# The first token group of a fused attention and MoE kernel: two products in plain float32 on whole weights, the fp32r halves of the weights made later, and conversion and loads spread anew

## Chip, cores and metric

One core of a Trainium2 chip runs the whole program. The metric is the device time of one execution in microseconds (us). The kernel before has a median of 759.26 us over three runs (758.15 to 760.97).

## What is computed

Three layers in a row, for 2 x 768 tokens of 8 heads of 64, that is 1536 tokens of width 512:

```python
scores = scale * np.matmul(q, k.transpose(0, 1, 3, 2))          # causal window of 128, and 4 sinks
a = np.exp(scores - max); a = a / (a.sum() + 1e-9); x = a @ v    # attention

r = np.maximum(x @ w_in, 0.0)                                    # dense layer, 512 -> 2048 -> 512
x = (r * r) @ w_out

logits = x @ w_gate + np.log1p(np.exp(x @ w_noise)) * noise      # top 2 of 8 experts
out[mask] += weight * (np.maximum(x[mask] @ w1[e], 0.0) @ w2[e]) # 512 -> 1024 -> 512
```

`w_in` and `w_out` come as float64. The kernel has to make float32 of them on the chip, out of the integer words.

## The kernel before

The 1536 tokens are six groups of 256. `fast1` does attention and the dense layer, the class `Experts` the rest. Inside both the order of the instructions on each engine is the order of the code (`manual_schedule`): every engine takes its own instructions one after the other and waits at each for what it needs.

**The prologue** goes over the heads a = 0 to 10 (group 0 has heads 0 to 7, group 1 starts with 8). For each head `scores` (L237, plain float32, two matmuls) is followed by `soft`: the VectorE (DVE) adds the mask and takes the minimum (L255), the ScalarE (ACT) takes exp with its sum (L258). `norm_a` adds 1e-9 (L262) and takes the reciprocal (L264), `norm` multiplies (L276 on DVE, L274 on ACT; strings such as "da" say which engine takes which of the two tiles). `trans` turns the tile on the TensorE (PE), `trans_b` copies it out on ACT, `pv` multiplies with v (L313) for two heads at a time, and ACT copies the result to `xraw` (L315). In the text "the soft row" of a head or step is its first L255 row on DVE, which comes as soon as its scores are there and DVE is free. `keep_warm` puts some matmuls without a use between (L653).

**Steps n = 0 to 47** then interleave attention of head a = n + 11 with the dense layer: step n belongs to group g = n // 8 and weight part u = n % 8. In a step PE does in this order: `scores(a)`, `pv(n + 8)` if n is even, the first product `mm1(n + 1)` (L383), the transposes `trans(n + 10)`, the second product `mm2(n)` (L416). Where u = 7, `mm2(n)` comes ahead of the scores, since the next group's input has to be split first (`split_x`, L366 on ACT and L367 on DVE). `act` (ACT) takes relu and square of the first product's result, `act_b` (L403, L404) the rest of the square that the fp32r tile has lost.

**fp32r in three passes.** A product of two float32 tiles is made of three fp32r matmuls: high x high, high x rest, rest x high (`PASS`). So each weight lies in SBUF as a high half and a rest, in one tile `w` [128, 2, 1024] of a ring of 16: eight parts u of `win` and of `wout`. The ring's tiles are used again for the experts' weights from step 40 on. `prep` splits q and k in the same way from head 18 on (`qs`, `kk`; casts on ACT at L214 and L215, subtractions on DVE at L216 and L217); the 18 heads before take plain float32.

**Conversion.** `cv_load` loads half a weight part as integer words (`st`, 512 KB, three buffers, queue of SP). Three DVE instructions make float32 of it: "1" (L171), "2" (L174), "3" (L177). "H" then makes the two halves: the high one on ACT (L148), the rest on GpSimd (POOL, L149). The tables `C0` (prologue) and `C1` (steps 0 to 7) say where in a head or step each of these letters stands. Of the 32 half parts 11 and two thirds are converted in the prologue. In steps 0 to 5 POOL also makes the rest of the square.

From step 8 on, `range_load` reads the float64 weights once more in 32 pieces, one per step, into two buffers `rw`, and `range_check` takes a minimum of each. The experts' raw weights use the same two buffers later.

Of the kernel before, what the change touches and what calls it, by code (L numbers as in the profile page):

```python
# [26 lines left out]
C = 448  # L27
# [7 lines left out]
def build(tc, io):  # L35
# [3 lines left out]
    with root:  # L39
# [3 lines left out]
        ring = rst.enter_context(tc.tile_pool(name="ring", bufs=16))  # L43
        rgt = ExitStack()
        xg = dram.tile([XROWS, TR], F32, name="xg")
# [50 lines left out]
def fast1(tc, io, env):  # L96
    nc = tc.nc
    PE, ACT, DVE, POOL, SP = nc.tensor, nc.scalar, nc.vector, nc.gpsimd, nc.sync
    wk, ps, ring, consts = env["wk"], env["ps"], env["ring"], env["consts"]
# [52 lines left out]
    nxt, whole, split = {"1": 0, "2": 0, "3": 0}, [], set()  # L152

    def convert(todo):

        for c in todo:
            if c == "H":
                while whole:
                    cv_b(whole.pop(0))
                continue  # L160
# [6 lines left out]
            if c == "1":  # L167
                if hf == 0:
                    W[name, u] = ring.tile([128, 2, 1024], F32R, name="w")
                t = CV[i] = cvp.tile([128, 512], I32, name="cv", bufs=4)  # L170
# [4 lines left out]
            else:  # L175
                t = CV[i]
                DVE.scalar_tensor_tensor(t, wd[:, :, 0], 29, t, op0=OP.logical_shift_right, op1=OP.bitwise_or)  # L177
                CV[i] = t.bitcast(F32)
                del ST[i]
                whole.append(i)  # L180
# [120 lines left out]
    def pv(a):  # L301
# [3 lines left out]
        if h == 0:  # L305
# [68 lines left out]
    def mm1(n):  # L374
        g, u = divmod(n, 8)
        assert ("win", u, 1) in split
        x, w = XT[g], W["win", u]
        hp = ps.tile([128, 2, 256], F32, name="h")
        for f in range(2):
            i = 0  # L380
            for c in range(4):
                for a, b in PASS:
                    PE.matmul(hp[:, f], w[:, a, c * 256 + f * 128:c * 256 + f * 128 + 128], x[:, b, c],  # L383
# [4 lines left out]
    def act(n, first=False):  # L388
        hp = HP.pop(n)
        r = wk.tile([128, 512], F32, name="r", bufs=1)  # L390
        gt = wk.tile([128, 2, 512], F32R, name="gt", bufs=2)
# [6 lines left out]
        GT[n] = gt, r, first  # L398

    def act_b(n):  # L400
        gt, r, first = GT[n]
        if not first:
            DVE.tensor_tensor(r, r, r, op=OP.mult)  # L403
        (POOL if first else DVE).tensor_tensor(gt[:, 1], r, gt[:, 0].bitcast(F32), op=OP.subtract)  # L404
        GT[n] = gt

    def mm2(n):
# [3 lines left out]
        assert ("wout", u, 1) in split  # L411
        gt, w = GT.pop(n), W["wout", u]
        for f in range(2):
            for t in range(2):
                for i, (a, b) in enumerate(PASS):
                    PE.matmul(ACC[g][t], gt[:, a, f * 256 + t * 128:f * 256 + t * 128 + 128],  # L416
                              w[:, b, f * 512:f * 512 + 512],
# [172 lines left out]
    def a_mm1(u, half):  # L590
# [5 lines left out]
        for c in range(4):  # L596
            for a, b in PASS:
                PE.matmul(hp[:, f], w[:, a, c * 256 + f * 128:c * 256 + f * 128 + 128], x[:, b, c],
# [10 lines left out]
    def a_mm2(u):  # L609
# [3 lines left out]
        for f in range(2):  # L613
            for t in range(2):
                for i, (a, b) in enumerate(PASS):
                    PE.matmul(A["acc"][t], hh[:, a, f * 256 + t * 128:f * 256 + t * 128 + 128],
                              w[:, b, f * 512:f * 512 + 512],
# [16 lines left out]
    C0 = (("1", "", "2", ""),) + (("H31", "", "2", ""),) * 9 + (("H31", "", "2", "H132"),)  # L634
    H0, H1, H2 = "da", "ad", "dd"
    STEP = "3", "1", "2H", "132132"
    C1 = (STEP,) * 3 + (STEP[:3] + ("132132132",),) + (STEP,) * 2 + (("3", "1", "2H", "3H"),) * 2
    smv = {}
    HALF, V1 = 8, (2, 3, 4)
    W0, W1 = 8, (3,) * 6 + (2,) * 5  # L640

    with tc.manual_schedule():
# [15 lines left out]
        cv_load()  # L658
        cv_load()
        scores(0, True)  # L660
        make_masks()
        for a in range(A0):
# [8 lines left out]
            if a == 0:  # L671
                load_v(0)
                cv_load()
# [6 lines left out]
            if a == 8:  # L680
                split_x(0)
            if a + 1 < A0:
                trans(a)
            convert(C0[a][3])
            if a == 9:
                mm1(0)
            if a == 10:
                act(0, True)
# [12 lines left out]
        for n in range(48):  # L701
# [7 lines left out]
            if n == 8:  # L709
# [7 lines left out]
                ex.range_load(1)  # L717
            if g >= 1 and u == 0:
                rows(p)
            if first:  # L720
                convert("H")
# [593 lines left out]
```

## Time and profile before

The profiled execution took 761.03 us; its span, which the trace covers, is 759.2 us.

| stretch, us from the span's start | what | PE busy | DVE busy | POOL busy |
|---|---|---|---|---|
| 0 to 49.29 | prologue | 38.74 | 38.68 | 17.24 |
| 49.29 to 125.05 | steps 0 to 6, and the second product of 7 | 64.81 | 74.57 | 52.35 |
| 125.05 to 169.46 | step 7 to the first product in step 13 | 44.07 | 30.57 | 4.54 |
| 169.46 to 189.12 | to the first product in step 15 | 19.66 | 15.13 | 4.25 |
| 189.12 to 759.2 | groups 2 to 5, experts | 556.16 | 312.81 | 96.88 |

A stretch in which one engine is busy for nearly its whole length is set by that engine, as long as no other one makes it wait. Busy time is not work alone: an instruction that is held up while it runs counts as busy.

### The profile page before, as it was taken

The numbers are of one execution on the slowest core, as the hardware profiler recorded it, in microseconds if no ns is written. First come the engines' busy times: TensorE is split into PE (matmuls) and PEld (weight loads), VectorE is DVE, ScalarE is ACT, GpSimd is POOL, SyncE is SP. The second block draws the span as 40 slices with busy tenths as digits, with TensorE's granted clock in tenths as the row PEclk, the third lists the DMA queues.
The fourth block names the chain that finished last, engine by engine and source line by source line (L and its number), as shares of the span: only waits on it lengthen the run. The fifth ranks groups of instructions, "written<-read, shape, count | busy, mean of one in ns | idle before, by whom it ended". The sixth has DMA issues, their size and how long they took to land.

```text
span 759.2 us, 12296 instructions
## 1 busy us (share of the span) xinstructions
PE 723.4 (95%) x4448; PEld 638.9 (84%) x4448; DVE 471.8 (62%) x1156; ACT 352.6 (46%) x741; POOL 175.3 (23%) x313
## 2 busy tenths in 40 slices
PE   7878879999999999999999999999999999999995
PEld 3467657988888888888898878899999999999994
DVE  6899998677768768766464445544554445455511
ACT  3675556564565555555254415333344433334410
POOL 1377563112002102301202022201112030303032
PEclk6799999999999999999999999999999999999998
DMA  8765576855756422622325027635556464646233
GB/s 230 222 207 179 191 250 221 280 198 175 246 169 227 167 101 96 215 94 84 114 84 170 1 91 240 210 111 156 141 160 156 148 169 134 172 137 165 74 43 46
DMA packets 37734, 119.05 MB, mean 157 GB/s; under 512 B 5038, under 2 KB 5166, under 8 KB 37408
## 3 DMA queue, kind: packets, MB, share of 16 engines
q1 hardware_dynamic: 31584, 104.37, 41.9%
q0 software_dynamic: 5792, 13.28, 8.5%
q8 instruction: 37, 0.61, 0.3%
q10 hardware_dynamic: 288, 0.52, 0.2%
q14 instruction: 33, 0.27, 0.1%
HBM read 104.88 MB, written 24.91 MB: 171 GB/s over the span
## 4 chain that ended last, share of the span: by engine, by line
PE 75%; DVE 12%; DMA 5%; issue 3%; ACT 2%; POOL 1%; SPq 0%; DVEq 0%; POOLq 0%; ACTq 0%
PE h L1001 18%; PE h L383 12%; PE acc L416 12%; PE acc L1027 7%; PE s L1027 7%; DVE cv L177 3%; PE o L313 2%; PE acc L1024 2%; PE s L241 2%; PE s L1024 1%; DVE cv L174 1%; DVE cv L171 1%; DMA xg<-xr,sx 1%; DVE pr L255 1%; DMA qk<-in_qk 1%
## 5 line engine op out<-in xcount | busy, mean ns | idle before, releaser
L416 PE MATMUL acc<-w,gt 128*128 128x512 f32 x576 | 149.5, 408 | 12.1 <-POOL gt L404 8.6
L383 PE MATMUL h<-xt,w 128*128 128x256 f32 x1152 | 148.9, 285 | 1.8 <-POOL w L149 1.5
L383 PEld LDWEIGHTS h<-xt,w 128*128 128x128 f32 x1152 | 140.5, 188 | 6.6 <-issue 3.2
L416 PEld LDWEIGHTS acc<-w,gt 128*128 128x128 f32 x576 | 106.5, 192 | 38.2 <-POOL gt L404 10.7
L1001 PE MATMUL h<-xt,w 128*128 128x448 f32 (+6 forms) x672 | 134.4, 349 | 0.0
L1001 PEld LDWEIGHTS h<-xt,w 128*128 128x128 f32 x672 | 123.3, 188 | 3.0
L906 DVE TENSOR_TENSOR w<-rw,w 128x1024 fp32r<-128x1024 f32 x64 | 78.4, 1225 | 37.7 <-ACT w L905 37.6
L1008 DVE SCALAR_TENSOR_TENSOR hh<-h,hh 128x256 fp32r<-128x256 f32 (+7 forms) x60 | 33.9, 565 | 108.1 <-ACT hh L1007 106.7
L1007 ACT ACTIVATE hh<-h 128x256 fp32r<-128x256 f32 (+7 forms) x60 | 29.8, 496 | 148.4 <-PE h L1001 148.4
L258 ACT ACTIVATE pr<-pr,mxall 128x264 f32<-128x264 f32 (+1 forms) x96 | 46.8, 489 | 74.5 <-DVE mxall L255 69.3
L975 POOL DMA_INDIRECT out<-x2t,mi x15 | 22.7, 1515 | 235.3 <-DVE x2t L1052 235.3
L1027 PE MATMUL acc<-hh,w 128*128 128x448 f32 (+5 forms) x288 | 72.7, 360 | 0.0
L905 ACT CAST w<-rw 128x1024 fp32r<-128x1024 f32 x64 | 67.1, 1049 | 10.1 <-DMA rw<-in_w 10.1
L1027 PE MATMUL s<-hh,w 128*128 128x448 f32 (+5 forms) x288 | 69.8, 350 | 0.0
L392 ACT ACTIVATE r<-h 128x512 f32<-128x512 f32 x48 | 28.6, 595 | 62.2 <-PE h L383 59.0
L149 POOL TENSOR_TENSOR w<-cv,w 128x512 fp32r<-128x512 f32 x32 | 45.8, 1432 | 47.5 <-ACT w L148 46.5
L1027 PEld LDWEIGHTS s<-hh,w 128*128 128x128 f32 x288 | 53.4, 188 | 1.2
L282 POOL COPY psk<-pr 128x8 f32<-128x8 f32 x64 | 23.8, 375 | 127.7 <-DVE pr L276 123.0
L1027 PEld LDWEIGHTS acc<-hh,w 128*128 128x128 f32 x288 | 51.1, 188 | 1.1
L255 DVE CUSTOM_DVE_ANT_0 pr<-s,masks 128x264 f32<-128x264 f32 (+1 forms) x96 | 35.4, 403 | 23.1 <-PE s L241 19.1
L403 DVE TENSOR_TENSOR r<-r 128x512 f32<-128x512 f32 x41 | 28.3, 690 | 28.7 <-ACT gt L397 28.7
L547 POOL DMA_INDIRECT xg<-xr,sx x24 | 26.1, 1086 | 43.0 <-DVE r L403 18.4
(238 smaller groups left out, 1084.0 us busy)
## 6 DMA issues: line engine op xcount, KB each, us to landing
rw<-in_w SPq DMA_DIRECT2D x64, 512.0 KB, 3.4
qk<-in_qk SPq DMA_DIRECT2D x40, 328.0 KB, 4.8
st<-in_win SPq DMA_DIRECT2D x16, 512.0 KB, 3.9
st<-in_wout SPq DMA_DIRECT2D x16, 512.0 KB, 4.5
rw<-in_win SPq DMA_DIRECT2D x16, 512.0 KB, 4.4
rw<-in_wout SPq DMA_DIRECT2D x16, 512.0 KB, 4.0
xg<-in_xg SPq DMA_DIRECT2D x8, 924.0 KB, 6.0
xr<-xg SPq DMA_DIRECT2D x24, 231.0 KB, 4.6
```

Source lines behind the costliest of these rows:

```text
L149: POOL.tensor_tensor(w[:, 1, sl], tf, w[:, 0, sl].bitcast(F32), op=OP.subtract)
L255: DVE.tensor_tensor_reduce(pt, SB[a][t][:, lo:hi], masks[:, t if gl == 0 else 2 + t, lo:hi], scale=-0.0625 if a in PLAIN and a >= HALF els ...
L258: ACT.activation(pt, pt, AF.Exp, bias=mx, scale=-1.0, accum_out=sm[:, t:t + 1])
L383: PE.matmul(hp[:, f], w[:, a, c * 256 + f * 128:c * 256 + f * 128 + 128], x[:, b, c], start=i == 0, stop=i == 11)
L392: ACT.activation(r, hp.rearrange("p a b -> p (a b)"), AF.Relu)
L416: PE.matmul(ACC[g][t], gt[:, a, f * 256 + t * 128:f * 256 + t * 128 + 128], w[:, b, f * 512:f * 512 + 512], start=u == 0 and f == 0 and i ...
L905: nc.scalar.copy(w[:, 0], t)
L906: nc.vector.tensor_tensor(w[:, 1], t, w[:, 0].bitcast(F32), op=OP.subtract)
L1001: PE.matmul(hp[:, :ncol], w[:, a, o:o + 128], XT[k][:, b, c, :ncol], start=i == 0, stop=i == 11)
L1007: ACT.activation(hh[:, 0, :ncol], hp[:, :ncol], AF.Relu)
L1008: DVE.scalar_tensor_tensor(hh[:, 1, :ncol], hp[:, :ncol], 0.0, hh[:, 0, :ncol].bitcast(F32), op0=OP.max, op1=OP.subtract)
L1027: PE.matmul(acc[:, :n], w[:, a, o + j * 128:o + j * 128 + 128], hh[:, b, :n], **st)
```

## The change

- In group 0 (steps 0 to 7) `mm1` and `mm2` take plain float32 operands: the whole weights `RAW`, the attention output `xraw[0]` and a float32 `gt`. The compiler makes two PE instructions of each such matmul. `split_x(0)`, the rest of the square and its third ACT instruction are gone in this group. `xraw[0]` lies in the buffer of `xt`.
- The ring's tiles are two, `w` (high) and `wl` (rest) of [128, 1024], 16 each. The converted weights lie in `wl` tiles (the last of them in a new buffer `spare`). `half_1` makes the high half on ACT at the end of steps 0 to 7, one instruction for a whole part, two a step. `half_2` makes the rest on DVE at the end of steps 6 to 13, two a step. POOL makes no halves any more.
- Conversion: two of the three DVE letters per head in the prologue (three in heads 9 and 10), twelve per step in steps 0 to 5, none later. `st` has four buffers, and four pieces are loaded ahead of the first head; v of group 0 is loaded first of all, from ACT's queue.
- `norm` takes both tiles on ACT in steps 0 to 15 ("aa").
- q and k are loaded with 64 rows up to head 17 (`HALF`, 8 before).
- `range_load` has one buffer; the experts' raw weights use it and `spare` in turn.

```diff
+        def halves():
+            return ring.tile([128, 1024], F32R, name="w"), ring.tile([128, 1024], F32R, name="wl")
...
-            st = cvp.tile([128, 512], I64, name="st", bufs=3)
+            st = cvp.tile([128, 512], I64, name="st", bufs=4)
...
-    def cv_b(i):
-        name, u, hf = cvs[i]
-        w, sl, tf = W[name, u], slice(hf * 512, hf * 512 + 512), CV.pop(i)
-        ACT.copy(w[:, 0, sl], tf)
-        POOL.tensor_tensor(w[:, 1, sl], tf, w[:, 0, sl].bitcast(F32), op=OP.subtract)
-        split.add(cvs[i])
...
+    def half_1(name, u):
+        t = W[name, u] = [ring.tile([128, 1024], F32R, name="w")]
+        ACT.copy(t[0], RAW[name, u])
+
+    def half_2(name, u):
+
+        t = ring.tile([128, 1024], F32R, name="wl")
+        DVE.tensor_tensor(t, RAW.pop((name, u)), W[name, u][0].bitcast(F32), op=OP.subtract)
...
+        if g == 0:
+            assert ("win", u, 1) in made
+            w = RAW["win", u]
+            for f in range(2):
+                for c in range(4):
+                    PE.matmul(hp[:, f], w[:, c * 256 + f * 128:c * 256 + f * 128 + 128],
+                              xraw[0][:, c], start=c == 0, stop=c == 3)
+            HP[n] = hp
+            return
...
-        if first:
-            ACT.activation(r, r, AF.Square)
-            ACT.copy(gt[:, 0], r)
-        else:
+        if n < 8:
             ACT.activation(gt[:, 0], r, AF.Square)
...
+                    PE.matmul(ACC[g][t], gt[:, 0, o:o + 128], w[:, f * 512:f * 512 + 512],
+                              start=u == 0 and f == 0, stop=u == 7 and f == 1)
...
-    C0 = (("1", "", "2", ""),) + (("H31", "", "2", ""),) * 9 + (("H31", "", "2", "H132"),)
-    H0, H1, H2 = "da", "ad", "dd"
-    STEP = "3", "1", "2H", "132132"
-    C1 = (STEP,) * 3 + (STEP[:3] + ("132132132",),) + (STEP,) * 2 + (("3", "1", "2H", "3H"),) * 2
+    C0 = (("", "1", "2"), ("", "3", "1"), ("", "2", "3")) * 3 + (("1", "2", "3"),) * 2
+    H0, H1, H2 = "da", "aa", "dd"
+    C1 = (("12", "3", "123", "123123"),) * 6 + (("12", "3", "", ""),) * 2
...
-    HALF, V1 = 8, (2, 3, 4)
+    HALF, V1 = 18, (2, 3, 4)
...
-        cv_load()
-        cv_load()
+        load_v(0)
+        for i in range(4):
+            cv_load()
...
-            if a == 8:
-                split_x(0)
...
-                norm(a, smv[a], H1 if first else H2)
+                norm(a, smv[a], H1 if n < 16 else H2)
...
+            if first:
+                half_1("win", u)
+                half_1("wout", u)
+            if 6 <= n < 14:
+                half_2("win", n - 6)
+                half_2("wout", n - 6)
...
-        self.range_load(i + 2)
+        self.range_load(i + 1)
```

DVE from the end of step 7 to the soft row of step 8, before (L262 and L264 end the softmax, L276 is a norm, `sel` and `xr` belong to step 8, `r` and `gt` are `act_b(8)`):

```order
L262 TENSOR_SCALAR sm<-sm 128x2
L264 RECIPROCAL sm<-sm 128x2
L276 TENSOR_SCALAR pr<-pr,sm 128x264
L216 TENSOR_TENSOR qs<-qk,qs 64x256
L217 TENSOR_TENSOR kk<-qk,kk 128x400
L714 TENSOR_REDUCE sel<-ident 128x16
L426 COPY xr<-acc 128x512
L403 TENSOR_TENSOR r<-r 128x512
L404 TENSOR_TENSOR gt<-r,gt 128x512
L255 ISA pr,mxall<-s,masks 128x264
```

The same place now (the lines have other numbers; `wl` is `half_2`):

```order
L270 TENSOR_SCALAR sm<-sm 128x2
L272 RECIPROCAL sm<-sm 128x2
L224 TENSOR_TENSOR qs<-qk,qs 64x256
L225 TENSOR_TENSOR kk<-qk,kk 128x400
L159 TENSOR_TENSOR wl<-wl,w 128x1024 x2
L739 TENSOR_REDUCE sel<-ident 128x16
L457 COPY xr<-acc 128x512
L424 TENSOR_TENSOR r<-r 128x512
L425 TENSOR_TENSOR gt<-r,gt 128x512
L263 ISA pr,mxall<-s,masks 128x264
```

The norm has left DVE, and two subtractions of 1024 columns stand between `kk` and the rest of the square, so ahead of the next soft row.

ACT in step 8, before, from the two exp on (`qs` and `kk` are the casts of `prep`, L392 and L397 are `act(9)`):

```order
L258 ACTIVATE pr,sm<-pr,mxall 128x264 x2
L315 COPY xraw<-o 128x256
L214 CAST qs<-qk 128x256
L215 CAST kk<-qk 128x400
L392 ACTIVATE r<-h 128x512
```

The same place now:

```order
L266 ACTIVATE pr,sm<-pr,mxall 128x264 x2
L326 COPY xraw<-o 128x256
L282 ACTIVATE pr<-pr,sm 128x264 x2
L222 CAST qs<-qk 128x256
L223 CAST kk<-qk 128x400
L412 ACTIVATE r<-h 128x512
```

Both norms stand ahead of the casts for which DVE's `qs` and `kk` wait.

SP's queue at the program's start, before (`qk` are the heads' q and k, 164 KB each here):

```order
L63 DMA nw<-in_nw 128x4
L190 DMA qk<-in_qk 64x656 x2
L141 DMA st<-in_win 128x512 x2
L190 DMA qk<-in_qk 64x656
L141 DMA st<-in_wout 128x512
```

And now:

```order
L68 DMA nw<-in_nw 128x4
L198 DMA qk<-in_qk 64x656 x2
L146 DMA st<-in_win 128x512 x2
L146 DMA st<-in_wout 128x512 x2
L198 DMA qk<-in_qk 64x656 x2
```

The third head's q and k stand behind four pieces of weights in place of two.

## Rows read from the trace of the kernel before

**Rows 1.** Busy time by stretch: length, then each engine's busy us.

```profile
49.29:125.05 75.76, 64.81 (x380) 52.07 (x379) 74.57 (x125) 44.66 (x97) 52.35 (x47) 0.95 0.65 218
125.05:169.46 44.41, 44.07 (x328) 39.07 (x327) 30.57 (x96) 27.53 (x67) 4.54 (x13) 1.00 0.62 213
169.46:189.12 19.66, 19.66 (x123) 16.44 (x123) 15.13 (x51) 8.21 (x23) 4.25 (x12) 1.00 0.55 193
```

**Rows 2.** Waits of PE from 40 to 125 us: total, times, longest.

```profile
PE acc L416 <- POOL gt L404: 8.6, 5, 2.7
```

**Rows 3.** POOL in order of time: start, duration, line.

```profile
73.00 1.74 POOL L404 TENSOR_TENSOR gt<-r,gt 128x512 fp32r<-128x512 f32 x1
```

**Rows 4.** DVE in order of time.

```profile
21.97 0.29 DVE L255 CUSTOM_DVE_ANT_0 pr<-s,masks 128x128 f32<-128x128 f32 x1
...
42.96 0.42 DVE L255 CUSTOM_DVE_ANT_0 pr<-s,masks 128x264 f32<-128x264 f32 x1
...
45.74 0.43 DVE L255 CUSTOM_DVE_ANT_0 pr<-s,masks 128x264 f32<-128x264 f32 x1
...
73.52 1.25 DVE L262 TENSOR_SCALAR sm<-sm 128x2 f32<-128x2 f32 x1
...
77.33 0.68 DVE L177 SCALAR_TENSOR_TENSOR cv<-st,cv 128x512 int32<-128x512 int32 x1
...
125.50 0.43 DVE L255 CUSTOM_DVE_ANT_0 pr<-s,masks 128x264 f32<-128x264 f32 x1 [0.47 <-PE s L241]
...
127.11 0.17 DVE L262 TENSOR_SCALAR sm<-sm 128x2 f32<-128x2 f32 x1 [0.82 <-ACT pr L258]
...
128.88 0.58 DVE L217 TENSOR_TENSOR kk<-qk,kk 128x400 fp32r<-128x400 f32 x1
...
130.13 0.69 DVE L403 TENSOR_TENSOR r<-r 128x512 f32<-128x512 f32 x1
...
131.47 0.42 DVE L255 CUSTOM_DVE_ANT_0 pr<-s,masks 128x264 f32<-128x264 f32 x1
...
161.11 0.43 DVE L255 CUSTOM_DVE_ANT_0 pr<-s,masks 128x264 f32<-128x264 f32 x1 [1.27 <-PE s L241]
```

**Rows 5.** PE in order of time (L237: scores; L383, L416: the products).

```profile
37.83 1.06 PE L237 MATMUL s<-qk 128*128 128x264 f32 x4
38.73 0.59 PE L653 MATMUL acc<-ones 128*128 128x512 bf16 x2
...
49.29 1.05 PE L237 MATMUL s<-qk 128*128 128x264 f32 x4
...
71.15 3.11 PE L383 MATMUL h<-xt,w 128*128 128x256 f32 x24
...
74.45 3.04 PE L416 MATMUL acc<-w,gt 128*128 128x512 f32 x12
77.32 1.05 PE L237 MATMUL s<-qk 128*128 128x264 f32 x4
...
125.05 0.65 PE L241 MATMUL s<-kk,qs 128*128 128x264 f32 x4
...
169.46 3.09 PE L383 MATMUL h<-xt,w 128*128 128x256 f32 x24
...
189.12 3.01 PE L383 MATMUL h<-xt,w 128*128 128x256 f32 x24
```

**Rows 6.** Chain of waits at the start: start, length, what.

```profile
5.37 5.88 DMA qk<-in_qk
```

**Rows 7.** Busy time from 6 to 12 us; last: PE clock, DMA share, GB/s.

```profile
6.00:12.00 6.00, 3.91 (x13) 2.00 (x14) 4.54 (x19) 3.35 (x11) 0.83 (x4) 0.61 0.98 302
```

**Rows 8.** Groups of instructions: busy us, mean ns, idle before.

```profile
L906 DVE TENSOR_TENSOR w<-rw,w 128x1024 fp32r<-128x1024 f32 x64 | 78.4, 1225 | 37.7 <-ACT w L905 37.6
```

**Rows 9.** ACT in order of time: the norm of step 7.

```profile
127.58 0.52 ACT L274 ACTIVATE pr<-pr,sm 128x264 f32<-128x264 f32 x1 [0.50 <-DVE sm L264]
```

**Rows 10.** Waits of PE from 122 to 210 us: total, times, longest.

```profile
PE o L504 <- DVE ohb L494: 0.2, 1, 0.2
```

More of the change, by code (lines that the diff above doesn't have):

```diff
@@ L175, in convert @@
             else:
-                t = CV[i]
+                t = CV.pop(i)
                 DVE.scalar_tensor_tensor(t, wd[:, :, 0], 29, t, op0=OP.logical_shift_right, op1=OP.bitwise_or)
-                CV[i] = t.bitcast(F32)
                 del ST[i]
-                whole.append(i)
+                made.add(cvs[i])
                 cv_load()
@@ L304, in pv @@
         b, gl = divmod(g, 3)
-        if h == 0:
+        if a == 0:
+            xraw[0] = wk.tile([128, 2, 4, 256], F32, name="xt", bufs=1)[:, 0]
+        elif h == 0:
             xraw[g] = wk.tile([128, 4, 256], F32, name="xraw", bufs=1)
@@ L386, in mm1, with act @@
         HP[n] = hp
-    def act(n, first=False):
+    def act(n):
         hp = HP.pop(n)
         r = wk.tile([128, 512], F32, name="r", bufs=1)
-        gt = wk.tile([128, 2, 512], F32R, name="gt", bufs=2)
+        gt = wk.tile([128, 2, 512], F32 if n < 8 else F32R, name="gt", bufs=2)
         ACT.activation(r, hp.rearrange("p a b -> p (a b)"), AF.Relu)
-        if first:
-            ACT.activation(r, r, AF.Square)
-            ACT.copy(gt[:, 0], r)
-        else:
+        if n < 8:
             ACT.activation(gt[:, 0], r, AF.Square)
-        GT[n] = gt, r, first
+            GT[n] = gt
+            return
+        ACT.activation(gt[:, 0], r, AF.Square)
+        GT[n] = gt, r
     def act_b(n):
[L401 to L404, printed above, removed]
+        if n < 8:
+            return
+        gt, r = GT[n]
+        DVE.tensor_tensor(r, r, r, op=OP.mult)
+        DVE.tensor_tensor(gt[:, 1], r, gt[:, 0].bitcast(F32), op=OP.subtract)
         GT[n] = gt
@@ L410, in mm2 @@
             ACC[g] = [ps.tile([128, 512], F32, name="acc") for _ in range(2)]
-        assert ("wout", u, 1) in split
-        gt, w = GT.pop(n), W["wout", u]
+        gt = GT.pop(n)
+        if g == 0:
+            assert ("wout", u, 1) in made
+            w = RAW["wout", u]
+            for f in range(2):
+                for t in range(2):
+                    o = f * 256 + t * 128
+                    PE.matmul(ACC[g][t], gt[:, 0, o:o + 128], w[:, f * 512:f * 512 + 512],
+                              start=u == 0 and f == 0, stop=u == 7 and f == 1)
+            return
+        assert ("wout", u) in split
+        w = W["wout", u]
         for f in range(2):
@@ L903, in weights @@
             t = self.raw.pop(k)
-            w = self.env["ring"].tile([128, 2, 1024], F32R, name="w")
-            nc.scalar.copy(w[:, 0], t)
-            nc.vector.tensor_tensor(w[:, 1], t, w[:, 0].bitcast(F32), op=OP.subtract)
+            w = self.env["halves"]()
+            nc.scalar.copy(w[0], t)
+            nc.vector.tensor_tensor(w[1], t, w[0].bitcast(F32), op=OP.subtract)
             self.W[k] = w
@@ L911, in range_load @@
             name, u, q = ("win", "wout")[i // 16], i % 16 // 2, i % 2
-            t = self.late.tile([128, 1024], F32, name="rw", bufs=2).bitcast(I64)
+            t = self.late.tile([128, 1024], F32, name="rw", bufs=1).bitcast(I64)
             self.rng[i] = t
@@ L950, in turn @@
             if k:
-                self.XT[k] = self.wk.tile([128, 2, 4, C], F32R, name="xt")
-            else:
-                self.XT[k] = env["ring"].tile([128, 2, 1024], F32R, name="w").rearrange(
-                    "p a (c n) -> p a c n", c=4)
+                t = self.wk.tile([128, 2, 4, C], F32R, name="xt")
+                self.XT[k] = t[:, 0], t[:, 1]
+            else:
+                self.XT[k] = [t.rearrange("p (c n) -> p c n", c=4) for t in env["halves"]()]
         r, c0, n = self.XR.pop((k, j))
@@ L1000, in mm1 @@
                 for a, b in PASS:
-                    PE.matmul(hp[:, :ncol], w[:, a, o:o + 128], XT[k][:, b, c, :ncol], start=i == 0, stop=i == 11)
+                    PE.matmul(hp[:, :ncol], w[a][:, o:o + 128], XT[k][b][:, c, :ncol], start=i == 0, stop=i == 11)
                     i += 1
             if k == E - 1 and f >= TAIL:
-                hh = env["ring"].tile([128, 2, 1024], F32R, name="w")[:, :, :C]
+                hh = env["halves"]()
             else:
                 hh = wk.tile([128, 2, C], F32R, name="hh", bufs=2)
-            ACT.activation(hh[:, 0, :ncol], hp[:, :ncol], AF.Relu)
-            DVE.scalar_tensor_tensor(hh[:, 1, :ncol], hp[:, :ncol], 0.0, hh[:, 0, :ncol].bitcast(F32),
+                hh = hh[:, 0], hh[:, 1]
+            ACT.activation(hh[0][:, :ncol], hp[:, :ncol], AF.Relu)
+            DVE.scalar_tensor_tensor(hh[1][:, :ncol], hp[:, :ncol], 0.0, hh[0][:, :ncol].bitcast(F32),
                                      op0=OP.max, op1=OP.subtract)
```

51 lines of the change are left out of this document (23 added, 28 removed).

## The prediction

> **What bounds the kernel now.** I read the busy times by stretch first, because the change touches only the first 190 us. From step 7 on PE is busy for 44.07 of 44.41 and 19.66 of 19.66 us, so PE sets the pace there and DVE has room, 30.57 of 44.41 [rows 1]. In steps 0 to 6 it is the other way round: DVE is busy for 74.57 of 75.76 us and PE for 64.81 [rows 1]. The waits of PE name the second product waiting for POOL's rest of the square, 8.6 us in five waits, the longest 2.7 [rows 2]. The DVE and POOL timelines show that DVE's fullness is not all work: the L262 row takes 1.25 us at 73.52 and 0.17 at 127.11, for the same 128x2 tile [rows 4], and the long one begins while POOL's subtraction of 73.00 to 74.74 runs [rows 3]. So POOL's 512-column subtractions hold up DVE, and DVE (late weights) and POOL (late squares) hold up PE. The low clock is in this too: PE's mean granted clock is 0.95 there [rows 1], which is some 7 us at the lower of its two levels.
>
> I go along PE's line: the scores of step 0 at 49.29, of step 7 at 125.05, the first product in step 13 at 169.46, the first product in step 15 at 189.12 [rows 5]. Each part below says how much later or earlier PE is at the next of these marks.
>
> **Prologue, up to 49.29.** Taken away: the 11 or 12 POOL subtractions and ACT casts, the split of group 0, about a third of the conversions. Added: a queue at the start. The load of head 2's q and k took 5.88 us from 5.37, to 11.25 [rows 6], while the DMA engines were 98% busy at 302 GB/s [rows 7]. It now stands behind two more pieces of 524 KB; 1.05 MB at 302 GB/s are 3.5 us. The 0.52 MB of v moved ahead of it were partly in the way before, so I add nothing for them. Heads 2 and 3 are paced by PE at its lower clock (0.61 in the mean from 6 to 12 us [rows 7]), so they move with the load, and the soft row of head 4 goes from 21.97 [rows 4] to about 25.5. From there a head costs what its own chain costs. The cleanest head before took 2.78 us (42.96 to 45.74) with three conversion instructions, two of which lay in DVE's wait for exp [rows 4]. Now there are two, but both after the exp, where nothing hides them: 2.7 to 3.0 for heads 4 to 7, 3.3 for heads 8 and 9, 17.9 for the six. The soft row of head 10 comes at 43.4. Then 0.45 for the transposes and 3.55 for the first product of step 0 bring its scores to 47.4: **1.9 us earlier**. Ends: 4 earlier, if v's early load and the clock help; 3 later, if PE falls to its lower level for two more stretches as before.
>
> **Steps 0 to 6, 49.29 to 125.05.** The waits for POOL go, and DVE is freed of the hold-ups. Its own work in a step is now twelve conversion instructions, the eight longer ones of 0.68 as at 77.33 [rows 4], the four others of some 0.4, 7.1 us at most, and about 1.2 for the softmax: up to 8.3 us. That is a little less than the 8.2 to 9.3 that PE will need, so PE sets the pace. The square's third ACT instruction goes, a norm comes to ACT, and the high halves are two casts of 1024 columns a step in place of three of 512; ACT was busy for 44.66 of 75.76 us [rows 1], and its idle time takes the half us or so that this adds. If that cover were gone, exp would come later, and DVE after it; the high halves stand behind the step's other ACT work, which speaks against it. Loads: four pieces a step, 2.1 MB, and half of q and k in about 8.7 us are 260 GB/s, under the 302 shown [rows 7]; the fourth buffer gives each some 7 us.
>
> PE pays for this. A float32 matmul is two instructions; four of 264 columns took 0.90 us up to the next start (37.83 to 38.73 [rows 5]), 0.225 each. Sixteen of 256 or eight of 512 columns are then 3.49 us per product; I take 3.55 for the weight changes. Before it was 2.94 for the first product (71.15 to 74.45, less 0.36 for the transposes) and 2.87 for the second (74.45 to 77.32) [rows 5]. The surplus is 0.61 and 0.68. PE's line without waits: 64.81 busy, less 3.4 for 7 us at the lower clock, is 61.4; adding the steps' own starts one by one gives 59.6. With 7 x 0.61 and 8 x 0.68, 9.7 in all, that is 69 to 71; I take 70.0, **5.7 us less** than 75.76. Ends: 8 less with the products at 3.4 and no waits, 1 less with the price below.
>
> The rows say 3.5 us for a float32 product of this size. The Trainium skill ("FP8 and Floating Point Precision", TensorE Precision Notes) says that true FP32 takes four passes through the array, where the three-pass product takes three; four thirds of 2.94 and 2.87 would be 3.9 and 3.8, 4.8 us more over the stretch. That would make the whole 7.3 slower; the scores of this trace speak against it, since their float32 columns cost less per pass than the fp32r ones.
>
> **Step 7 to the first product in step 13, 125.05 to 169.46.** Here DVE gets the rests. One 1024-column subtraction takes 1.225 us [rows 8]; two, the second behind the first, 2.4, in each of steps 6 to 13. Two norms a step leave DVE (0.6). By busy time it would fit: 30.57 + 6 x 2.4 - 3.3 is 41.7 of 44.4. But the chain decides. From the soft row at 125.50 to the end of `kk` at 129.46 it is 3.96 us, with waits for ACT inside (exp, then norm and cast) [rows 4]; a second norm on ACT ahead of the casts adds 0.4 (the one there takes 0.52 [rows 9]). Then come the two subtractions, 2.4, which can't start earlier, since DVE takes its instructions in order; then the square's rest, 1.34 (130.13 to 131.47 [rows 4]); then the next soft row. That makes 8.1 us a step, where PE's line took 44.41 for six steps, 7.4 each. Step 7 has two more instructions of step 8 in it (0.7): 8.8. Step 9 copies a tile on DVE, step 10 one on ACT: 8.4 and 8.2; step 11 8.2. Step 12 took 8.35 from its soft row at 161.11 to PE's 169.46 and had DVE's routing at its end, which PE already waited for by 0.2 [rows 4, 5, 10]; with 2.4 and the norms on ACT it is 11.0. The sum is 8.8 + 8.1 + 8.4 + 8.2 + 8.2 + 11.0 = 52.7, against 43.96 from 125.50 to 169.46: **8.7 us more**. PE waits at the scores for `kk`, in step 9 at the transposes for DVE's copy out of their bank, and most of all in step 13 for the routing's one-hot rows. Ends: 0 (all hidden, by the busy sum) and 11.
>
> **Steps 13 and 14, 169.46 to 189.12.** Step 13 has the last two subtractions, and both steps both norms on ACT. DVE was already full in step 13. Its lag makes the rest of the square of step 15 come about 1.2 us after the second product there wants it: **1.4 more**, ends 0 and 3.
>
> **The rest** is unchanged: norms on DVE again from step 16; the checked weights' one buffer is filled right after each check and has a step's time; the ring turns as before. 0, ends -0.5 and 1.
>
> **Sum.** -1.9 - 5.7 + 8.7 + 1.4 = +2.5 us. The profiled execution took 761.03 (span 759.2, 1.8 around it) and would take 763.5. It is 1.8 above the median of the runs, 759.26; on the median I say **761.8**.
>
> **The rivals.**
> *The rests are hidden.* Then the third and fourth terms shrink to 0.5, and the time is 759.3 - 1.9 - 5.7 + 0.5 = 752.2. For it: DVE's busy sum fits under PE's line, and PE has a lead of two score banks. Against it: the in-order chain above, each link of which has its row. Chance 0.18.
> *The clock falls again.* PE waits about 4 us for step 13's routing and idles at the start behind the longer queue. The trace has 7 us at the lower level in steps 0 to 6 [rows 1] and more in the prologue. Two more such stretches cost 3.4 us each at most where PE sets the pace; about 4.5 in all, 766.3. It decides as soon as PE idles for over 2 us twice. Chance 0.14; this is the one that ends clearly slower.
> *Four full passes.* The float32 products cost 3.9 and 3.8, +4.8: 766.6. Chance 0.07, because of the scores' row; the Trainium skill's page cited above is what speaks for it.
> *It doesn't free PE.* The weights of steps 1 to 6 still come late, since fewer are converted in the prologue and the loads need 260 GB/s: some 4 us of the 5.7 are lost, 765.8. Chance 0.08.
>
> **How the numbers follow.** My forecast, 761.8, has 0.53; its own range is 757 to 767. Half a percent, 3.8 us, is about what a measurement of this kernel tells from no change: faster is under 755.5, slower over 763.1. Of the forecast's 0.53 I give 0.02 to faster, 0.38 to the same, 0.13 to slower. Hidden rests: 0.16 faster, 0.02 the same. Clock: 0.11 slower, 0.03 the same. Four passes: 0.06 and 0.01. Not freed: 0.05 and 0.03. Together 0.18 faster, 0.47 the same, 0.35 slower. The range 754 to 768 leaves out most of the hidden case and little above.
>
> **What would show it.** In the profile after: the scores of step 0 near 47.4; no wait of PE for POOL; float32 products of 3.5 us from start to start; steps 0 to 5 of 8.2 to 9.3 us with DVE under 90% busy and no L262 row over 0.3; soft rows of steps 8 to 11 some 8.2 us apart; waits of PE for `kk` and one of 3 to 5 us for the one-hot rows; from step 16 on steps as before. If the soft rows of steps 8 to 12 follow the scores at 0.4 us, my third term is wrong. If PE waits for `made` weights in steps 1 to 5, my second is. If the scores of step 0 come after 50, my first is.

## The result and the profile after

The changed kernel takes 767.97 us (median of four executions, 765.68 to 770.91), 1.0106 times the kernel before, which now has a fourth execution and a median of 759.99 (95% interval 1.0068 to 1.0144). Timed again on another occasion it took 767.85, 1.0096 times (1.0068 to 1.0124). That is some 8 us slower. I had said 761.8 and "the same"; the range, 754 to 768, just holds it.

Both kernels were profiled twice. The marks are those of the prediction, on PE's line:

| stretch | before | before, second trace | after | after, second trace | change, predicted |
|---|---|---|---|---|---|
| prologue, to the scores of step 0 | 49.29 | 49.70 | 52.97 | 55.13 | -1.9 |
| to the scores of step 7 | 75.76 | 74.46 | 69.73 | 69.73 | -5.7 |
| to the first product in step 13 | 44.41 | 44.44 | 53.30 | 53.30 | +8.7 |
| to the first product in step 15 | 19.66 | 19.65 | 20.99 | 21.17 | +1.4 |
| to the end of the span | 570.08 | 569.95 | 566.81 | 567.27 | 0 |
| span | 759.2 | 758.2 | 763.8 | 766.6 | +2.5 |

The first trace of after is of an execution of 765.68 us, the fastest of its four; the second is of one of 768.41, the longest of its six but only 0.6 above their median. So the second one is the typical sum: +5.6, -5.4, +8.9, +1.5, -2.7 against the means of the two traces of before, 7.9 us in all. The term that failed is the first: the prologue became longer instead of shorter.

The stretches of the first trace of after, in the columns of [rows 1] (length, busy us of PE, PE's weight loads, DVE, ACT, POOL, then PE's granted clock, DMA share, GB/s):

```profile
0.00:52.97 52.97, 42.60 (x158) 21.83 (x158) 27.69 (x115) 23.48 (x70) 4.22 (x24) 0.77 0.58 177
52.97:122.70 69.73, 69.73 (x292) 44.62 (x291) 54.44 (x125) 43.51 (x89) 3.95 (x14) 1.00 0.76 241
122.70:176.00 53.30, 46.51 (x330) 39.37 (x328) 40.32 (x97) 33.77 (x80) 2.80 (x13) 1.00 0.48 170
176.00:196.99 20.99, 20.99 (x124) 17.77 (x122) 16.29 (x49) 9.60 (x27) 4.25 (x12) 0.93 0.42 147
```

Against [rows 1], steps 0 to 6 have turned round: PE is busy for the whole of 69.73 us, all of it at the upper level of its clock, and DVE for 54.44. In the third stretch PE now has 6.8 us without work, and DVE is busy for 40.32 of 53.30: no engine is full, so something waits in a row.

DVE in that stretch, from the soft row of step 8 to that of step 9:

```profile
132.43 0.43 DVE L263 CUSTOM_DVE_ANT_0 pr<-s,masks 128x264 f32<-128x264 f32 x1
...
135.75 0.42 DVE L224 TENSOR_TENSOR qs<-qk,qs 64x256 fp32r<-64x256 f32 x1 [1.34 <-ACT qs L222]
136.21 0.58 DVE L225 TENSOR_TENSOR kk<-qk,kk 128x400 fp32r<-128x400 f32 x1
136.70 2.48 DVE L159 TENSOR_TENSOR wl<-wl,w 128x1024 fp32r<-128x1024 f32 x2
139.09 0.68 DVE L424 TENSOR_TENSOR r<-r 128x512 f32<-128x512 f32 x1
...
140.42 0.43 DVE L263 CUSTOM_DVE_ANT_0 pr<-s,masks 128x264 f32<-128x264 f32 x1
```

The step is 7.99 us from soft row to soft row. In it DVE waits 1.34 us for ACT's cast of q, and then the two subtractions, 2.48 us, stand between `kk` and the square. The waits of DVE there (123 to 172 us), and those of PE (122.7 to 176):

```profile
DVE qs L224 <- ACT qs L222: 8.2, 6, 1.5
```

```profile
PE o L535 <- DVE ohb L525: 3.0, 1, 3.0
```

The second line is the one of [rows 10], 0.2 before.

The prologue. PE's scores of heads 2, 6, 7, 8, 9, 10 and of step 0, in the first trace of after:

```profile
14.33 0.89 PE L245 MATMUL s<-qk 64*128 64x128 f32 x4 [2.54 <-DMA qk<-in_qk]
...
27.93 0.92 PE L245 MATMUL s<-qk 64*128 64x128 f32 x4
...
32.56 1.61 PE L245 MATMUL s<-qk 64*128 64x128 f32 x4 [1.35 <-DMA qk<-in_qk]
...
37.38 2.12 PE L245 MATMUL s<-qk 64*128 64x264 f32 x4
...
41.04 2.13 PE L245 MATMUL s<-qk 64*128 64x264 f32 x4
...
46.26 1.16 PE L245 MATMUL s<-qk 64*128 64x264 f32 x4
...
52.97 1.15 PE L245 MATMUL s<-qk 64*128 64x264 f32 x4
```

The same instruction tells the level of the clock: four scores of 128 columns take 0.92 us or 1.61 to 1.65, four of 264 columns 1.15 or 2.13. Heads 4 to 6 come 2.8 to 2.9 us apart (22.25, 25.05, 27.93). Then PE waits 1.35 us for the q and k of head 7, and the next heads run at the lower level, 4.8, 3.7 and 5.2 us apart. In the second trace it is head 8 that waits, and the lower level follows there. (The profile puts this wait down to DVE's L180, but no score reads what L180 writes; the load of head 8 went out at 34.69, 5.2 us earlier.)

```profile
39.91 1.13 PE L245 MATMUL s<-qk 64*128 64x264 f32 x4 [2.13 <-DVE wl L180]
...
41.83 2.12 PE L245 MATMUL s<-qk 64*128 64x264 f32 x4
```

Why a load of 164 KB comes late, DVE's third conversion instruction and SP's queue show (first trace of after; the third row of SP is head 7's load):

```profile
25.79 0.69 DVE L186 SCALAR_TENSOR_TENSOR wl<-st,wl 128x512 int32<-128x512 int32 x1
```

```profile
26.51 0.33 SPq L146 DMA_DIRECT2D st<-in_wout  x1
26.89 0.42 SPq L213 DMA_DIRECT2D vs<-in_vs  x1
27.41 0.47 SPq L198 DMA_DIRECT2D qk<-in_qk  x1
```

Head 7's load goes out at 27.41, and the scores want it from about 31.2; such a load takes 5.0 us to land in the median of the first 40 us. There are two buffers, so a load can't go out until the head two before it has its scores, here head 5 at 25.97. It then stands behind a packed weight tile, which waits until DVE has converted an earlier piece, at 26.48, and behind `vs`. That place in the queue costs it 1.4 us, about what PE waits.

### The profile page after: what moved, and what is told of

Its sections match the earlier page's. It is cut to its first block, busy times and chain, and to the rows that moved or that the text cites. A ratio compares the mean times of both kernels' runs of the same rounds, so it can differ in the third digit from the quotient of the medians.

```text
span 763.8 us, 12017 instructions
## 1 busy us (share of the span) xinstructions
PE 734.4 (96%) x4352; PEld 633.0 (83%) x4352; DVE 450.8 (59%) x1142; ACT 353.9 (46%) x738; POOL 111.7 (15%) x274
## 5 line engine op out<-in xcount | busy, mean ns | idle before, releaser
L403 PE MATMUL h<-xt,w 128*128 128x256 f32 x640 | 119.7, 288 | 0.0
L447 PE MATMUL acc<-w,gt 128*128 128x512 f32 x320 | 109.1, 404 | 2.5 <-DVE gt L425 2.5
L935 DVE TENSOR_TENSOR wl<-rw,w 128x1024 fp32r<-128x1024 f32 x64 | 78.4, 1225 | 40.4 <-ACT w L934 39.5
L403 PEld LDWEIGHTS h<-xt,w 128*128 128x128 f32 x640 | 99.5, 190 | 3.2 <-issue 2.3
L403 PE MATMUL h<-xt,wl 128*128 128x256 f32 x320 | 90.6, 283 | 0.0
L1030 PEld LDWEIGHTS h<-xt,w 128*128 128x128 f32 x448 | 83.1, 188 | 2.2
L1030 PE MATMUL h<-xt,wl 128*128 128x448 f32 (+6 forms) x224 | 78.1, 349 | 0.0
L447 PEld LDWEIGHTS acc<-w,gt 128*128 128x128 f32 x320 | 59.9, 188 | 16.2 <-DVE gt L425 3.7
L447 PE MATMUL acc<-wl,gt 128*128 128x512 f32 x160 | 62.9, 393 | 0.0
L403 PEld LDWEIGHTS h<-xt,wl 128*128 128x128 f32 x320 | 60.9, 190 | 0.0
L412 ACT ACTIVATE r<-h 128x512 f32<-128x512 f32 x48 | 28.6, 595 | 60.1 <-PE h L403 50.4
L1057 PE MATMUL acc<-hh,w 128*128 128x448 f32 (+5 forms) x192 | 54.6, 365 | 0.0
L1030 PEld LDWEIGHTS h<-xt,wl 128*128 128x128 f32 x224 | 42.0, 188 | 0.8
```

Of the source, the lines that this page charges most:

```text
L403: PE.matmul(hp[:, f], w[a][:, c * 256 + f * 128:c * 256 + f * 128 + 128], x[:, b, c], start=i == 0, stop=i == 11)
L935: nc.vector.tensor_tensor(w[1], t, w[0].bitcast(F32), op=OP.subtract)
L1030: PE.matmul(hp[:, :ncol], w[a][:, o:o + 128], XT[k][b][:, c, :ncol], start=i == 0, stop=i == 11)
L1057: PE.matmul(acc[:, :n], w[a][:, o + j * 128:o + j * 128 + 128], hh[b][:, :n], **st)
```

## The experiments

**One subtraction in the gap** (`e1_gap`), on the changed kernel. DVE waits for the cast of q in every step; a subtraction of 1.22 us fits into that.

```diff
                 norm(a, smv[a], H1 if n < 16 else H2)
+                if 6 <= n < 14:
+                    half_2("win", n - 6)
...
-                half_2("win", n - 6)
                 half_2("wout", n - 6)
```

> One thing moved: in steps 6 to 13 the first of VectorE's two 1024-column subtractions stands right behind the norm, ahead of the next head's key difference, where VectorE waits 1.34 us a step for ScalarE's cast of the queries; the second stays at the end of the step. Theory 1 (steps 7 to 12 run at the pace of VectorE's row of instructions, 8.1 to 8.8 us a step): a step falls to 7.0 to 7.3 us, the stretch from step 7 to step 13 falls from 53.3 to 46 to 47 us, TensorE's 3.0 us wait for the one-hot rows in step 13 goes or falls under 1 us, and the whole is 6 to 8 us under the changed kernel, near 760. Rival (the steps are paced by ScalarE's row or by the loads of the expert weights): the stretch stays above 51 us, the whole within 2 us of the changed kernel.

Measured: 759.91 us, 8.0 less, level with the kernel before (1.0001, 0.9977 to 1.0026). The stretch is 47.03 us, 6.3 less. DVE's step (133.03 to 139.77) is 6.74:

```profile
134.93 1.21 DVE L159 TENSOR_TENSOR wl<-wl,w 128x1024 fp32r<-128x1024 f32 x1
136.36 0.42 DVE L224 TENSOR_TENSOR qs<-qk,qs 64x256 fp32r<-64x256 f32 x1 [0.23 <-ACT qs L222]
136.81 0.58 DVE L225 TENSOR_TENSOR kk<-qk,kk 128x400 fp32r<-128x400 f32 x1
137.31 1.22 DVE L159 TENSOR_TENSOR wl<-wl,w 128x1024 fp32r<-128x1024 f32 x1
```

DVE's wait for ACT fell from 8.2 to 1.5 us, PE's wait for the one-hot rows from 3.0 to 1.7 (not under 1, as theory 1 had it), and the next stretch from 21.0 to 19.71 with it. Theory 1 holds: the order of DVE's row set the pace, not the amount of its work, which is the same (39.99 us busy against 40.32).

**The norms on DVE again** (`e4_norm`). The edit takes in steps 8 to 15; those of 8 to 12 lie in the stretch.

```diff
-                norm(a, smv[a], H1 if n < 16 else H2)
+                norm(a, smv[a], H1 if first else H2)
```

> From step 8 to step 12 both halves of the norm stand on VectorE again, as in the kernel before, instead of on ScalarE. The prediction's price for the move was a loss: ScalarE's two 128x264 scalings stand ahead of its casts of the next queries and keys, for which VectorE then waits 1.34 us a step. Theory 1 (casts come earlier by about two scalings, 0.9 us, and VectorE works 0.5 us more itself): steps 8 to 12 shorten by 0.2 to 0.5 us each, the stretch from step 7 to step 13 falls from 53.3 to 51 to 52.3 us. Rival (VectorE's own work is what counts): each step grows by 0.4 to 0.6 us, the stretch is 55 to 56 us.

One execution, 762.74 us, so only its stretches are compared. The stretch is 49.99, 3.3 less, more than either theory said: DVE does 3.2 us more work (43.56 busy), and its wait for ACT's casts all but goes:

```profile
DVE qs L224 <- ACT qs L222: 1.3, 1, 1.3
```

So moving work to the engine with more room lengthened the chain, because it moved ahead of what the other engine waits for. It is the same wait that `e1_gap` fills.

**The old order of the first loads** (`e2_loads`).

```diff
-        load_v(0)
-        for i in range(4):
-            cv_load()
+        cv_load()
+        cv_load()
...
+            if a == 0:
+                load_v(0)
+                cv_load()
+            if a == 1:
+                cv_load()
```

> The loads at the start stand in the old order again: two packed weight tiles ahead of the first scores, the values and a third tile in head 0, a fourth in head 1. Theory 2a (the start is longer because head 2's queries and keys queue behind four packed tiles and the values): head 2's scores at 12 to 12.5 us instead of 14.3, the first scores of step 0 at 50 to 51 instead of 52.97, the whole 2 to 3 us less. Theory 2b (the start is longer because later, at heads 6 to 8, TensorE waits for queries and keys that have two buffers, and the clock falls from 32 to 46 us): the head start is lost again there, step 0 stays at 52 to 53.5, the whole within 1 us.

763.69 us, 4.2 less (1.006 times before, 1.004 to 1.008). The first scores come at 4.46 instead of 7.05, those of head 2 at 11.33, those of step 0 at 47.32. The traced execution is the fastest of its ten, 761.05 us. PE still waits at head 7, 1.50 us, but the clock is at the lower level only from 31.0 to 34.5 us, against 32.2 to 45.9 in the changed kernel (granted clock 0.50 in both), and the scores of head 8 already run at the upper one:

```profile
30.43 1.05 PE L245 MATMUL s<-qk 64*128 64x128 f32 x4 [1.50 <-DMA qk<-in_qk]
...
34.60 1.15 PE L245 MATMUL s<-qk 64*128 64x264 f32 x4
```

Head 4's scores come 2.1 us earlier (20.19), step 0 5.7: the other 3.6 us are this shorter stretch. So the gain is larger than theory 2a said, and not lost as 2b said. Why the clock came back so soon here is open. So the wait of 1.50 us cost less of the clock here than that of 1.35 in the changed kernel.

**A third buffer for q and k in the prologue** (`e3_qk3`).

```diff
-        t = wk.tile([128, 256 + KW], F32, name="qk", bufs=2)
+        if a % 3 == 2 and a < 12:
+            t = spare.tile([128, 1024], F32, name="rw0")[:, :256 + KW]
+        else:
+            t = wk.tile([128, 256 + KW], F32, name="qk", bufs=2)
...
+        load_qk(2)
...
-            load_qk(a + 2)
+            if a + 3 < 13:
+                load_qk(a + 3)
```

> In the start alone the queries and keys have a third buffer (the spare tile, which stands empty until step 5), and each head's load stands one head earlier. Theory 2b (two buffers are too few: a load takes 4.5 to 5.1 us, two heads take 5.4, and TensorE waits 1.35 us at head 7 and 1.08 before it, whereupon the clock is low from 32 to 46 us): these waits go, the clock stays at its upper level from 32 to 46 us, step 0 begins at 47 to 48.5 instead of 52.97, the whole is 4 to 6 us less. Theory 2c (the clock falls there whatever the loads do): the waits go and the low windows stay, step 0 at 51 to 52.5, the whole 1 to 2 us less. Theory 2a: only head 2 comes earlier, by 2 us, step 0 at 51.

761.02 us, 6.8 less (1.0013, 0.999 to 1.0036). After the first head PE waits for no load, the scores of heads 7 to 9 last 0.92 to 1.16 us, from head 4 on heads come 2.7 to 3.4 us apart, and step 0 begins at 45.75. That is theory 2b. All traces bear it out: in the five with two buffers (the changed kernel twice, `e1_gap`, `e2_loads`, `e4_norm`) PE waits 1.35 to 2.13 us at head 7 or 8 and a stretch at the lower level follows; in the six with three and every load in time (this one, and `x1_late7` and the `c` kernels below) there is neither. The steps from 0 on are as in the changed kernel (69.73 and 53.33).

**That load late again** (`x1_late7`, `x2_later7`), to see whether the lower clock hangs on the wait.

```diff
-            if a + 3 < 13:
+            if a + 3 < 13 and a + 3 != 7:
                 load_qk(a + 3)
+            if a == 5:
+                load_qk(7)
```

> e3_qk3 with one load put back: the queries and keys of head 7 are asked for one head later, behind those of head 8, and nothing else is touched. TensorE should wait 1 to 2.5 us ahead of head 7's scores, as in the changed kernel. Theory 2b (this wait is what brings the clock down to its lower level over the next heads): rows of the scores of heads 7 to 9 last 1.6 to 2.1 us instead of 0.9 to 1.2, and step 0 begins at 49 to 53 us instead of 45.75: 2 us or more beyond the wait itself. Theory 2c (the low stretch from 32 to 46 us has another cause and e3_qk3 escaped it by luck): the rows stay short and step 0 begins at 46.5 to 48.5 us.

764.06 us, 3.0 more than `e3_qk3`, but the trace decides nothing: in that execution the first stretch at the lower level lasted to 30 us instead of 20, heads 2 to 5 were slow, head 7's load came in time, and step 0 began at 49.07. The second kernel has the same load at the end of head 5.

> In x1_late7's profiled execution head 7's load came in time, because the clock was low up to 30 us and heads 2 to 5 ran slowly. Here that load stands at the end of head 5, behind a packed weight tile, so that TensorE must wait 3 to 5 us ahead of head 7's scores, whether the first low stretch ends at 20 or at 30 us. Theory 2b (a wait of TensorE there brings the clock down): rows of the scores of heads 7 to 9 at 1.6 to 2.1 us instead of 0.9 to 1.2, for at least 6 us; step 0 begins at 45.75 (49.1 after a long first stretch) plus the wait plus 2 us or more. Theory 2c (the low stretch at 32 to 46 us does not hang on waits): the rows of heads 7 to 9 stay at 0.9 to 1.2 us, step 0 begins at 45.75 or 49.1 plus the wait alone.

769.86 us, 8.8 more than `e3_qk3`. The scores of heads 6 to 10 and of step 0:

```profile
26.80 0.92 PE L248 MATMUL s<-qk 64*128 64x128 f32 x4
...
35.00 1.61 PE L248 MATMUL s<-qk 64*128 64x128 f32 x4 [4.92 <-DMA qk<-in_qk]
...
39.82 2.13 PE L248 MATMUL s<-rw 64*128 64x264 f32 x4
...
43.48 2.13 PE L248 MATMUL s<-qk 64*128 64x264 f32 x4
...
49.02 2.12 PE L248 MATMUL s<-qk 64*128 64x264 f32 x4
...
57.08 1.16 PE L248 MATMUL s<-rw 64*128 64x264 f32 x4
```

Up to head 6 this execution runs as `e3_qk3` did (its head 6 was at 26.89). The wait is 4.92 us, step 0 is 11.3 later: 6.4 us beyond the wait, all heads in between at the lower level. So this late load cost its wait and then the clock, as theory 2b said. How much of the lower clock a shorter wait brings is not fixed by this: `e2_loads` had only 3.4 us of it after 1.50.

**Where the spread comes from** (`e0_same`, the changed kernel again; `b0_again`, the kernel before again).

> The changed kernel as it is, timed again beside the others on the same chip. Its runs so far lie 5 us apart (765.7 to 770.9) while the kernel before stays within 3. Theory A (the spread is a property of this kernel: the clock falls in some executions in places where the engine stands idle): a median of 766 to 770 again, runs 2 to 5 us apart, and a profile whose stretches differ from the first profile's by whole windows of the lower clock. Theory B (that one chip was uneven): the runs lie within 2 us of 765.

The two traces of after differ by 2.8 us in the span and by 2.16 in the prologue; the stretches from step 0 to step 13 agree within 0.01. So the spread sits in the prologue, in how long PE's clock stays low there. The first such stretch begins before 10 us in all traces and ends near 20 us in some and near 30 in others (`e3_qk3` against `x1_late7`: 3.3 us in the start of step 0). These are the stretches of theory A. But such a spread is not the changed kernel's alone: 27 executions of the kernel before, timed beside these, lay between 757.30 and 762.30.

> The kernel before, profiled once more, to see which of its stretches are steady. If the 3 us that the changed kernel is shorter after step 15 come from the change, this trace has again about 570 us from the first product of step 15 to the end, with no half-clock window there. If they were one fall of the clock in the first profile (a window of 3.4 us near 418 us), this trace has 567 to 568 us there and the start and the steps 0 to 14 take 1 to 3 us more than in the first profile, since the total is about the same.

It has 569.95 us after step 15. So the 3 us that the changed kernel gains there are no accident of one trace of before; the fall of the clock is there in both. Near 418 us PE waits for the rest of the square, which stands on DVE behind a half of the experts' weights, and that behind a load. Before, and after:

```profile
419.16 2.36 PE L416 MATMUL acc<-w,gt 128*128 128x512 f32 x7 [3.03 <-DVE gt L404]
```

```profile
426.56 0.74 PE L447 MATMUL acc<-w,gt 128*128 128x512 f32 x2 [2.46 <-DVE gt L425]
```

The wait is 0.6 us shorter, and in the 5 us behind it the granted clock is 1.00 where it was 0.66 in both traces of before. From the one-hot product before that place to the next one it is 40.3 us in place of 42.4. But the shorter wait is not what spares the clock: `c4_three_dd` below waits 2.20 us there and `c3_early_dd` 2.68, and both have the fall (3.4 us at the lower level) and an end of 568.2 and 568.9 us; the ten traces of the changed kernel and its variants without it have 566.2 to 567.5. So up to 2 of the 3 us hang on whether the clock falls there, and why it mostly does not any more is open. The last 0.7 us or so I did not trace.

**All three mends** (`c1_three`: `e1_gap`, `e2_loads` and `e3_qk3`).

> The three edits of e1_gap, e2_loads and e3_qk3 together, on the changed kernel: one subtraction in the gap, the old order of the first loads, the third buffer for the queries and keys in the start. If the causes are separate, step 0 begins at 43 to 46 us, step 7 69.7 us later, steps 7 to 12 take 47 us, and the whole is 750 to 755 us, 0.7% to 1.2% under the kernel before. If the two edits of the start mend the same wait, step 0 begins at 45 to 47.5 us and the whole is 753 to 757.

748.72 us (747.80 to 751.01), 0.9861 times the kernel before (0.9833 to 0.9889): faster than both. The three gains, 8.0, 4.2 and 6.8, make 19.0; all together they are 19.1 to 19.3. As medians they add up. In the traces the gap's 6.3 us do too, but the two edits of the start do not quite: alone they bring step 0 forward by 5.7 and 7.2 us, together by 9.7, since both shorten or remove the same late stretch at the lower clock. Its stretches:

```profile
0.00:43.28 43.28, 37.28 (x158) 19.66 (x158) 27.02 (x115) 23.13 (x70) 4.23 (x24) 0.88 0.77 217
43.28:113.00 69.72, 69.72 (x291) 44.62 (x291) 54.30 (x125) 43.51 (x89) 4.21 (x14) 1.00 0.75 241
113.00:160.09 47.09, 44.77 (x330) 39.36 (x328) 39.98 (x97) 33.81 (x80) 4.19 (x13) 1.00 0.55 193
```

**Beyond it** (`c2_early`, `c4_three_dd`, `c3_early_dd`). The first puts `half_2` of six weights at the ends of steps 1 to 6, in the order in which the ring's buffers come free:

```diff
+    GAP2 = {6: (5,), 7: (7,), 8: (8,), 9: (10,), 10: (12,), 11: (13,), 12: (14,), 13: (15,)}
+    END2 = {1: (0,), 2: (1,), 3: (2,), 4: (3,), 5: (4,), 6: (6,), 8: (9,), 9: (11,)}
```

> As c1_three, and six of the sixteen subtractions stand in steps 1 to 6, one at the end of each, where VectorE is busy 44.6 of 69.7 us; ten are left for steps 6 to 13. Theory 1 (VectorE's row sets the pace of steps 7 to 12, TensorE that of steps 0 to 6): steps 0 to 6 stay at 69.7 us, steps 7 to 12 fall from 47 to 43 to 45 us, the wait for the one-hot rows in step 13 goes under 1 us, the whole is 2 to 4 us under c1_three. Rival (the subtractions put off VectorE's conversions and soft rows in steps 1 to 6): steps 0 to 6 grow by 1 us or more and eat the gain.

749.33 us (747.36 to 752.71), not to be told from `c1_three`. Steps 0 to 6 stay at 69.72 with DVE at 59.59 us; steps 7 to 12 take 45.86, 1.2 less, and PE waits 0.56 for the one-hot rows. Theory 1 had said 43 to 45, and 2 to 4 us for the whole; PE is busy for 44.66 of the 45.86, so little was left to gain. In this trace the first low stretch was the long one, and step 0 began at 46.61 instead of 43.28. The other two put the norms on DVE.

> c1_three and the norms of steps 8 to 12 on VectorE again; all sixteen subtractions in steps 6 to 13. With the subtraction in the gap VectorE's wait for ScalarE's casts is filled, so the 3.3 us that e4_norm gained by itself should be gone for the most part: the stretch from step 7 to step 13 is 46 to 48 us (47.1 in c1_three), the whole within 1.5 us of c1_three's 748.7. If the gain adds up instead, 44 us and 746.

752.98 us (0.9927, 0.9906 to 0.9948), 4 us worse than `c1_three`, where within 1.5 was expected. The stretch is 48.25, 1.2 more; only 1.5 us of waits for ACT's casts were left to remove, and DVE's work counts. PE then waits 2.25 us for the one-hot rows and is at its lower level after it, and the next stretch is 22.42 in place of 19.72.

> c2_early (the two mends of the start, a subtraction in the gap, six of the sixteen subtractions in steps 1 to 6) and, as in e4_norm, the norms of steps 8 to 12 on VectorE again. Theory 1 (VectorE still waits for ScalarE's casts there): the stretch from step 7 to step 13 falls from 45.9 to 43 to 45 us and the whole is 747 to 748.5 us. Rival (with VectorE's row relieved, its own two scalings a step now cost): the stretch is 46 to 48 us and the whole 749 to 751.

751.28 us (748.41 to 753.16); the stretch is 46.50, 0.6 more than in `c2_early`. The medians of these two, four executions each, can't be told apart, but the stretch speaks for the rival: what gains 3.3 us alone loses with the gap filled.

## Why the prediction was wrong, step by step

**Prologue: wrong.** The queue at the start was priced well: head 2's scores came 2.95 us later, at 14.33 for 11.38, where I had 3.5, and the soft row of head 4 at 24.37 for my 25.5. What failed is the next sentence, "from there a head costs what its own chain costs". I took 2.7 to 3.0 us from DVE's and ACT's work and never asked whether the loads keep that pace. A load takes about 5 us and two buffers cover two heads; at 2.7 us a head that leaves nothing for the place behind a packed weight tile. `e3_qk3` shows what the chain costs when the loads keep up: 22.4 us from head 4's soft row (23.33) to step 0 (45.75), for my 21.9, against 28.6 in the changed kernel (24.37 to 52.97). So the chain was sized well; the 6.2 us beyond it, a wait for a load and the lower clock behind it, stood in the sum at nothing. The start at 45.75 is even earlier than my 47.4. The clock was in the ends of this term (3 later) and in the second rival. That rival's 766.3 is near what was measured, in part by luck: it looked for the idle time in the first queue and in step 13, "as soon as PE idles for over 2 us twice". PE did (2.54 us at head 2, 2.96 in step 13), but the longest stretch at the lower level, 13.7 us, came behind the wait of 1.35 at head 7, which it did not name. It deserved more than 0.14.

**Steps 0 to 6: right.** -6.0 or -4.7 against the two traces of before, for -5.7. No wait for POOL is left, DVE is 78% busy, and PE has no gap. One pair of products of a step:

```profile
63.69 3.72 PE L393 MATMUL h<-xt,wl 128*128 128x256 f32 x16
67.24 0.27 PE L297 MATMUL pt<-ident,pr 128*128 128x128 f32 x1
...
67.68 3.60 PE L439 MATMUL acc<-wl,gt 128*128 128x512 f32 x8
71.21 1.15 PE L245 MATMUL s<-qk 64*128 64x264 f32 x4
```

The second product takes 3.53 us to the next start; the first takes 3.55, up to 67.24, where the next instruction starts. That is the 3.55 taken from the scores' row [rows 5]. The three-pass product took 2.94, so the ratio is 1.21, and the rival of 3.9 us is out. The Trainium skill ("FP8 and Floating Point Precision", TensorE Precision Notes) gives true FP32 four passes through the array; as an estimate at equal cost per pass that would be four thirds of 2.94, 3.9. The measurement decides: it does not speak against the four passes themselves, only against each costing as much as one of the three.

**Step 7 to step 13: right, and for its reason.** 53.30 us for 44.41, +8.9 for +8.7. The soft rows came 8.78, 7.99, 8.27, 8.14 and 8.11 us apart, and 11.06 to step 13's product, for my 8.8, 8.1, 8.4, 8.2, 8.2 and 11.0. All six are within 0.13, and they make 52.35 for 52.7; the first soft row came 0.95 us after step 7's scores, where it had come 0.45 after them, which makes up for it. `e1_gap` shows that the chain, not the busy sum, did it.

**Steps 13 and 14: the right size, the wrong reason.** +1.3 for +1.4. But PE waits nowhere for the rest of the square of step 15; it is the clock, 0.93 over this stretch, after the wait of 3.0 us for the one-hot rows. With that wait at 1.7 us (`e1_gap`) the clock is 1.00 and the stretch 19.71.

**The rest: wrong by 3 us.** I had an end of -0.5. PE's wait near 418 us became 0.6 shorter and the clock behind it mostly did not fall. One buffer fewer for the checked weights is the change that lies nearest, but no run tries it alone, so the cause is not shown. It was luck for the range: without these 2.7 us the median would by this sum have been near 771, outside the range.

**The other rivals.** The rests were not hidden, the weights were not late. That the prologue and steps 7 to 12 could be mended with a few lines the prediction didn't see: the gap of 1.34 us before `qs` was in its own chain as a cost.

## What to carry to other kernels

Where work on one engine gets shorter, check that the loads still keep its pace: time to land and place in the queue against the number of buffers times the new period. Put in-order work into a wait that recurs on its engine before counting whether there is room, and don't move an operation to a freer engine ahead of what others wait for. A wait of PE of a microsecond or two may be paid again by the clock behind it, so look at the rows of one repeated matmul after every such wait.

## What was new about the hardware

- PE's lower clock level outlasts the wait before it, by very different lengths. In the prologue there were 13.7 us of it with the wait of 1.35 us (after, head 7), 3.4 with 1.50 (`e2_loads`, head 7), 10.2 with 2.01 and 2.13 (`e1_gap` and the second trace of after, head 8) and 23.9 with 4.92 (`x2_later7`). At the one-hot rows of step 13 waits of 2.25 to 2.97 us brought 3.4 or 6.8 us of it in all eight traces, waits of 0.56 to 1.70 none in four. Near 418 us it did not fall after 2.46 (after) and did after 2.20 (`c4_three_dd`). The length of the wait alone does not decide, and what else does is open.
- The first stretch at the lower level, from before 10 us, is there in every trace, with little idle time ahead of it in `c1_three` and `c2_early`, and lasts to about 20 or about 30 us. This was not settled.
- In some traces the granted clock reads 1.00 over the first 20 us while four scores of 128 columns take 1.65 us. There the rows tell the level, not the column.
- A plain float32 matmul of 256 columns is two PE instructions and takes 0.444 us (3.55 for eight matmuls, 16 rows), against 0.1225 for one fp32r pass (2.94 for the same eight in 24 rows) and 0.368 for three.
